# Other visits for the conversion of w1 in the first attention

## Chip, cores, metric

One Trainium2 chip, one of its cores. The metric is the device time of one execution in microseconds (us); lower is better. Line numbers (L...) are those of the kernel before.

## The reference

Hash attention over 4 batches x 8 heads, 768 positions, head size 64, then a Fourier mixing block with a two-layer perceptron.

```python
q_bits = (q @ proj > 0); k_bits = (k @ proj > 0)        # 6 bits each
mask = bucket(q_bits)[:, :, :, None] == bucket(k_bits)[:, :, None, :]
scores = where(mask, q @ k.T / 8, -1e9)
attn = softmax(scores) @ v                              # (4, 8, 768, 64)
x = attn.transpose(0, 2, 1, 3).reshape(4, 768, 512)
u = x + real(fft(fft(x, axis=1), axis=2))
un = (u - mean(u)) / sqrt(var(u) + 1e-6)
out = u + relu(un @ w_ch1) @ w_ch2                      # 512 -> 2048 -> 512
```

w_ch1 (512 x 2048) and w_ch2 arrive as 64-bit floats and are narrowed to 32 bits on the chip.

## The kernel before

The kernel goes through the four batches. `attention(b)` handles a batch as four pairs of heads; pair n (n = 4b + t) is six steps, one for each block of 128 keys, c = 0 to 5, and after each step the generator yields. In this text such a yield of `attention(0)` is a **visit**: i = 6t + c, 24 of them.

A step does, for its block of keys: scores of all 768 queries for both heads (PE, L897 and L905), two halves g into two PSUM buffers; the exponential of each half (ACT, L916); the values of the step before (PE, L941); and a running sum of the exponentials (DVE, `acc`, L1026, not for c = 0 and c = 5). In the first five pairs the mask is put into the scores: the key and query bits, computed on PE (L812), are turned by DVE into the tile `qkb` (L816, L822, L828) and enter by the matmuls of L897. So the scores of pair n+1 cannot start before DVE has written its `qkb`.

The closing of pair n falls into steps 0 and 1 of pair n+1, function `scale`: after the last values, ACT copies the output out (L952, L955), PE sums the weights over the keys (L960), DVE turns that sum and takes its reciprocal (`rt`, `rc`: L967, L969, L970). One step later ACT spreads the reciprocal (`rr`, eight copies, L978) and DVE turns it again and multiplies (L983, L987).

`prepare(n+1)` runs inside pair n, one piece per step from c = 1: turn q (DVE, L779); the norm of q (ACT, L761, which reads the loaded q) and turn k; the norm of k, and the bits of q; the bits of k. `load(n+1)`, the DMAs for q (eight, L576), k (four, L568) and v (two, L562) of the next pair, is issued on SP's queue at the start of pair n. q and k of two pairs share buffers, so `load(n+1)` also needs that `prepare(n)` has finished reading.

Beside the attention runs `weights1`, the conversion of w1: 16 slices of 128 x 512, in the order f outer (four column blocks), c inner (four row blocks). Each `next` on it converts one slice (`narrow`): on DVE L639, L643 and, after ACT's L647, L649; on ACT L647, L654, L655. It then issues the fetch (SP, L704, 512 KB) of the slice seven further on, into the same raw buffer; there are seven raw buffers, three in the tile `zraw` and four in the tile `fraw`. `zraw` lies where `fold` later writes its `z` (from visit 21 on), `fraw` where `mix(0)` writes `F`. A fetch waits until DVE and ACT have read the buffer.

When the four slices of a column block f < 1024 are done, the next `next` starts `average(f)`: PE sums the block (`ws`, L664; four products, one for each row block, the last of which needs the last slice), ACT copies the sum (`part`, L669), and then the next slice is converted. The `next` after that does the mean (`wm`, PE, L672) and subtracts it (`centre`, DVE, L678, four operations) ahead of its slice. The two column blocks from 1024 on are averaged after the attention.

Which visit calls `next` is said in the main program: `if i % 5 < 4`. The part from `prepare(0)` to the late averages stands under `manual_schedule`, so each engine works through its instructions in the order in which the program issues them.

Of the kernel before, what the change touches and what calls it, by code (L numbers as in the profile page):

```python
# [26 lines left out]
NPAIR = H // 2  # L27
# [458 lines left out]
def _main(  # L486
# [27 lines left out]
    def wt(shape, dtype, tag, name, bufs=2):  # L514
        return work.tile(shape, dtype, tag=tag, name=name, bufs=bufs)
# [4 lines left out]
    def pt(shape, name):  # L520

        turn[0] += 1
        if roomy[0] and turn[0] % 2:
            if turn[0] % 4 == 1:
                return ps_o.tile(shape, F32, tag="o", name=name)
            return ps_sc.tile(shape, F32, tag="sc", name=name)
        return ps_1.tile(shape, F32, tag="ps", name=name)
# [147 lines left out]
    def centre(f, avg):  # L675
        for c in range(NDC):
            w = w1[:, c, f : f + WC]
            nc.vector.tensor_tensor(w, w, avg, op=ALU.subtract)  # L678
# [43 lines left out]
    def weights1():  # L722
        slices = [
            (w1[:, c, f : f + WC], moe_w_ch1[c * P : (c + 1) * P, f : f + WC])
            for f in range(0, DFF, WC)
            for c in range(NDC)
        ]
        zt = wt([P, 3, 2 * WC], F32, "z", "zraw1", 1)
        ft = wt([P, 12, WC], F32, "F", "fraw", 1)
        raws = [zt[:, i] for i in range(3)] + [  # L730
            ft[:, i : i + 2].rearrange("p i w -> p (i w)") for i in range(0, 8, 2)
        ]
        arrival = Arrival(slices, raws, 0, nc.sync)
        for i in range(arrival.depth):
            arrival.fetch(i)
            if i == 2:
                load(1)
        yield
        half = None
        for i in range(len(slices)):  # L740
            arrival.convert(i, ft[:, 8 + i % 4].bitcast(I32))
            yield
            if half:
                centre(half[0], next(half[1]))
                half = None
            if i % NDC == NDC - 1:


                f = i // NDC * WC
                if f < DFF // 2:  # L750
                    half = f, average(f)
                    next(half[1])
# [6 lines left out]
    def norm(n, io, tn):  # L759
        junk = wt([P, S], BF16, "junk", f"sq{io}_{n}", 1)  # L760
        nc.scalar.activation(  # L761
            junk, tn, AF.Square,
            accum_out=norms[:, io, n : n + 1],
        )

    def prepare(n):

        lite = n in LITE
        ts = {}
        for io, nm in enumerate("qk"):  # L770
            tn = nat.pop((nm, n))
            tt = wt([P, S], F32, nm + "t", f"{nm}t{n}")
            if n > 0:
                to, at = tt, tn
                if nm == "q":

                    to = tt.rearrange("p (i r n) -> p r i n", i=2, r=2)
                    at = tn.rearrange("p (r i n) -> p r i n", i=2, r=2)
                nc.vector.transpose(to, at)  # L779
            for g in range(2) if n == 0 else ():  # L780
                ps = pt([P, 3, P], f"tr{nm}{n}_{g}")
                for i in range(3):
                    c = 2 * i + g if nm == "q" else 3 * g + i
                    nc.tensor.transpose(ps[:, i, :], tn[:, c * P : (c + 1) * P], ident)
                if nm == "q":
                    for i in range(2):
                        dst = tt[:, i * HALF + g * HALF // 2 : i * HALF + (g + 1) * HALF // 2]
                        evac(
                            dst.rearrange("p (j c) -> p c j", c=3),
                            ps[:, :, i * D : (i + 1) * D],  # L790
                        )
                else:
                    evac(
                        tt[:, g * HALF : (g + 1) * HALF],
                        ps.rearrange("p c t -> p (c t)"),
                    )
            ts[nm] = tt
            yield
            norm(n, io, tn)
        if lite:  # L800

            qk = wt([P, 2, S], BF16, "qb", f"qkb{n}")
            qz = qk[:, 0].rearrange("p (g s) -> p g s", g=2)
            bits = {"q": qz[:, 0], "k": qk[:, 1, 0:HALF]}
            for io, nm in enumerate("qk"):
                ps = pt([P, HALF], f"bits{nm}{n}")
                for j in range(4):  # L810
                    h, g = divmod(j, 2)
                    nc.tensor.matmul(  # L812
                        ps[32 * j : 32 * j + 32, :], pjw[:, h * D : h * D + 32],
                        ts[nm][:, g * HALF : (g + 1) * HALF], start=True, stop=True,
                    )
                nc.vector.tensor_scalar(  # L816
                    bits[nm], ps, 0.0, off[:, io : io + 1],
                    op0=ALU.is_gt, op1=ALU.subtract,
                )
                if io == 0:  # L820
                    for g in (1, 0):
                        nc.vector.tensor_scalar(  # L822
                            qz[:, g], qz[:, 0], own[:, g : g + 1], None, op0=ALU.mult
                        )
                else:
                    for j in range(4):
                        to, at = (slice(32 * i, 32 * i + 32) for i in (j, j ^ 1))
                        nc.vector.tensor_copy(qk[to, 1, HALF:S], qk[at, 1, 0:HALF])  # L828
                yield
            preps[n] = ts["q"], ts["k"], qk, None  # L830
            return

        ps = pt([P, HALF], f"bits{n}")
        for j in range(4):
            src = ts["qk"[j // 2]][:, (j % 2) * HALF : (j % 2 + 1) * HALF]
            nc.tensor.matmul(
                ps[32 * j : 32 * j + 32, :], pj, src, start=True, stop=True
            )
        bt = wt([P, HALF], BF16, "bt", f"bt{n}")
        nc.vector.tensor_scalar(bt, ps, 0.0, None, op0=ALU.is_gt)  # L840
        yield

        qb = wt([P, 2, S], BF16, "qb", f"qb{n}")
        kb = wt([P, 2, NT], F32, "kb", f"kb{n}")
        for h in range(2):
            ps = ps_sc.tile([P, 2, 512], F32, tag="sc", name=f"qb{n}_{h}")
            for g in range(2):
                rows = slice(32 * g, 32 * g + 32)
                with behind() if g + h else nullcontext():
                    last[0] = nc.tensor.matmul(  # L850
                        ps[:, g, 0:HALF], pw[rows, h, :], bt[rows, :],
                        start=True, stop=True,
                    )
            evac(qb[:, h, :].rearrange("p (g s) -> p g s", g=2), ps[:, :, 0:HALF])
        ps = ps_sc.tile([P, 2, 512], F32, tag="sc", name=f"kb{n}")
        for c in range(NT):
            g, i = divmod(c, NT // 2)
            rows = slice(64 + 32 * g, 96 + 32 * g)
            with behind() if c else nullcontext():
                last[0] = nc.tensor.matmul(  # L860
                    ps[:, g, 2 * i : 2 * i + 2], bt[rows, i * P : (i + 1) * P],
                    pw[rows, :, 0], start=True, stop=True,
                )
        nc.vector.tensor_copy(
            kb.rearrange("p h (g i) -> p g i h", g=2),
            ps[:, :, 0:NT].rearrange("p g (i h) -> p g i h", h=2),
        )
        preps[n] = ts["q"], ts["k"], qb, kb
# [674 lines left out]
    with tc.manual_schedule(engines={ET.PE, ET.DVE, ET.Activation, ET.Pool, ET.SP}):  # L1543
        for _ in prepare(0):
            pass
        roomy[0] = False
        for i, _ in enumerate(attention(0)):
            if i == 2 * NT - 1:
                nc.sync.dma_start(ch, cn["ch"].ap())
                nc.sync.dma_start(sq, cn["sq"].ap())  # L1550
            if i % 5 < 4:
                next(other, None)
        for _ in other:
            pass
        pwf = wt([P, 2, P], F32, "ef", "pwf", 1)
        nc.sync.dma_start(pwf, cn["pw"].ap())
        nc.scalar.copy(pw, pwf)
        means = []
        late = [(f, average(f)) for f in range(DFF // 2, DFF, WC)]
        for _, avg in late:  # L1560
            next(avg)
        for f, avg in late:
            means.append((f, wt([P, WC], F32, "u", f"mean{f}", 2)))
            nc.scalar.copy(means[-1][1], next(avg))
# [94 lines left out]
```

## Time and profile before

| what | us |
|---|---|
| median of 3 runs | 1078.12 (1077.32 to 1079.49) |
| the profiled execution | 1079.54 |
| its span | 1077.8 |

So 1.74 us of the profiled execution lie around its span, and it is 1.42 us above the median. Over the span PE is busy 96%, DVE 73%, ACT 46%.

The first exponential of each pair of the first attention starts, in the timeline of ACT, at:

| pair | 0 | 1 | 2 | 3 | 4 (second attention) |
|---|---|---|---|---|---|
| us | 12.95 | 37.26 | 65.07 | 88.77 | 120.83 |

In the timeline a row gives start, length, engine, line, operation, output<-input, count, and in brackets how long the engine sat idle before it and what released it. Busy shares of a whole span mix stages with different limits: what a change in the first 120 us is worth is read there. A row of SPq is an issue of DMAs; its length is the time SP spent on issuing.

### The profile page before, as it was taken

The page shows a single profiled execution, that of the slowest core. Times are in us where ns is not written, and L with a number is a line of the kernel's source. Part 1 is how long each engine was busy: PE and PEld are TensorE (multiplying, and loading weights), DVE is VectorE, ACT ScalarE, POOL GpSimd, SP SyncE. Part 2 cuts the span into 40 slices and gives each one's busy share as a digit, 9 for nine tenths or more (in the row PEclk, how much of TensorE's full clock was granted, in tenths as well). Part 3 has the DMA queues.
Part 4 walks back from the last instruction along what each step waited for, and adds up shares of the span by engine and source line. Part 5 has one row for each costly group of instructions (what it writes and reads, how often), then busy time and mean ns, then how long its engine had stood idle before and what let it go on. Part 6 is the DMA issues. An engine that isn't in the chain of part 4 may idle for free.

```text
span 1077.8 us, 14130 instructions
## 1 busy us (share of the span) xinstructions
PE 1034.6 (96%) x4933; PEld 633.4 (59%) x4933; DVE 786.7 (73%) x1336; ACT 500.4 (46%) x1055; POOL 59.3 (5%) x132
## 2 busy tenths in 40 slices
PE   7989899999999999999999999999999999999997
PEld 3333364447644585545664575645675579668576
DVE  5899969896789977777858876776856875644353
ACT  6988554762287323455336424354325522440420
POOL 0000000011000020010000020010000012200000
PEclk9999999999999999999999999999999999999998
DMA  8764452370154461224062233222033204222301
GB/s 200 206 141 78 99 143 54 122 237 9 29 131 169 136 187 37 52 64 88 11 191 73 64 104 116 50 66 66 15 111 96 69 23 173 61 78 90 125 20 42
DMA packets 175710, 103.13 MB, mean 96 GB/s; under 512 B 129552, under 2 KB 162960, under 8 KB 175632
## 3 DMA queue, kind: packets, MB, share of 16 engines
q1 hardware_dynamic: 169840, 88.65, 30.6%
q0 software_dynamic: 4224, 13.11, 3.7%
q8 instruction: 41, 0.67, 0.3%
q10 hardware_dynamic: 1568, 0.39, 0.2%
q14 instruction: 37, 0.30, 0.1%
HBM read 81.14 MB, written 20.97 MB: 95 GB/s over the span
## 4 chain that ended last, share of the span: by engine, by line
PE 72%; DVE 17%; ACT 6%; issue 2%; DMA 1%; SPq 1%; DVEq 0%; ACTq 0%
PE o L1335 26%; PE h_p L1456 22%; PE oo L941 8%; PE sc L905 7%; DVE acc L1026 3%; DVE pk L930 2%; PE cs L1147 2%; ACT pk L916 2%; PE A L1176 2%; PE B L1176 1%; DMA kn<-in_k_dram 1%; ACT rr L978 1%; DVE x L1190 1%; PE sum L960 1%; SPq L576 1%
## 5 line engine op out<-in xcount | busy, mean ns | idle before, releaser
L1335 PE MATMUL o<-w,h 128*128 128x256 f32 x1152 | 260.0, 383 | 0.8 <-DVE w L1347 0.6
L1335 PEld LDWEIGHTS o<-w,h 128*128 128x128 f32 x1152 | 217.8, 191 | 41.8 <-issue 6.5
L916 ACT ACTIVATE pk<-sc 128x768 f32<-128x768 f32 x192 | 147.4, 809 | 78.2 <-PE oo L941 33.3
L1456 PE MATMUL h_p<-x,w 128*128 128x384 f32 x448 | 164.5, 494 | 3.1 <-ACT h L1478 1.6
L905 PE MATMUL sc<-qt,kt 64*128 64x384 f32 x768 | 154.9, 505 | 3.1 <-ACT pk L916 2.8
L930 DVE SCALAR_TENSOR_TENSOR pk<-qb,kb,pk 128x768 f32<-128x768 bf16 x132 | 128.7, 1012 | 39.0 <-ACT pk L916 38.4
L941 PE MATMUL oo<-pk,vn 128*64 128x385 f32 (+1 forms) x768 | 146.4, 495 | 1.1 <-DVE pk L930 0.6
L1456 PEld LDWEIGHTS h_p<-x,w 128*128 128x128 f32 x448 | 82.0, 190 | 69.3 <-issue 9.9
L1026 DVE TENSOR_TENSOR acc<-acc,pk 128x1536 f32<-128x1536 f32 (+1 forms) x72 | 105.8, 1483 | 5.3 <-ACT pk L916 5.1
L1456 PE MATMUL h_p<-w 128*128 128x384 f32 x288 | 106.1, 490 | 0.1
L941 PEld LDWEIGHTS oo<-pk,vn 128*64 128x64 f32 x768 | 50.5, 136 | 87.0 <-issue 72.6
L905 PEld LDWEIGHTS sc<-qt,kt 64*128 64x128 f32 x768 | 66.5, 187 | 55.7 <-issue 18.4
L1456 PEld LDWEIGHTS h_p<-w 128*128 128x128 f32 x288 | 53.6, 190 | 39.6 <-ACT w L1493 2.4
L1365 ACT COPY tq<-o 128x256 f32<-128x256 f32 x24 | 8.9, 373 | 104.8 <-PE o L1335 104.8
L1347 DVE SCALAR_TENSOR_TENSOR w<-o,rs,w 128x256 f32<-128x256 f32 x56 | 26.6, 479 | 41.2 <-PE o L1335 41.2
L1335 PE MATMUL o<-w 128*128 128x256 f32 x176 | 42.2, 383 | 0.2 <-DVE w L1347 0.2
L1489 DVE TENSOR_TENSOR h<-h 128x384 f32<-128x384 f32 x32 | 17.8, 555 | 29.6 <-ACT h L1488 29.6
L1085 POOL DMA_DIRECT2D out_dram<-w x30 | 16.4, 548 | 407.6 <-issue 314.6
L1335 PEld LDWEIGHTS o<-w 128*128 128x128 f32 x176 | 32.9, 190 | 7.5 <-DVE w L1347 1.2
L1354 ACT COPY tq<-o 128x256 f32<-128x256 f32 x24 | 8.8, 368 | 60.3 <-PE o L1335 60.1
L1381 DVE TENSOR_TENSOR tq<-tq,o 128x256 f32<-128x256 f32 x24 | 10.0, 418 | 36.4 <-PE o L1335 36.4
L1482 DVE TENSOR_TENSOR h<-h 128x384 f32<-128x384 f32 x32 | 17.7, 552 | 21.8 <-ACT h L1481 21.7
(170 smaller groups left out, 1334.5 us busy)
## 6 DMA issues: line engine op xcount, KB each, us to landing
w<-ad SPq DMA_DIRECT2D x168, 128.0 KB, 2.0
w<-bd SPq DMA_DIRECT2D x42, 512.0 KB, 4.4
zraw<-in_moe_w_ch_dram POOLq DMA_DIRECT2D x16, 512.0 KB, 4.4
bd<-w SPq DMA_DIRECT2D x14, 512.0 KB, 3.3
vn<-in_v_dram SPq DMA_DIRECT2D x32, 192.0 KB, 3.5
qn<-in_q_dram SPq DMA_DIRECT2D x120, 48.0 KB, 2.4
kn<-in_k_dram SPq DMA_DIRECT2D x60, 96.0 KB, 3.0
zraw<-in_moe_w_ch_dram SPq DMA_DIRECT2D x8, 512.0 KB, 7.4
```

Of the source, the lines that this page charges most:

```text
L905: last[0] = nc.tensor.matmul(ps[:, h, 0:HALF], kt[rows, ks], qt[rows, qs], start=kb is not None, stop=True,)
L916: done_by[ET.Activation] = nc.scalar.activation(pk[:, g, :, 0:HALF], ps[:, :, 0:HALF], AF.Exp, scale=SCALE)
L930: done_by[ET.DVE] = nc.vector.scalar_tensor_tensor(w, qb[:, h].rearrange("p (g s) -> p g s", g=2), kb[:, h, c : c + 1], w, op0=ALU.is_equa ...
L941: oo = nc.tensor.matmul(oos[g][h * D : (h + 1) * D, 0:w], nat["v", n][:, (2 * c + h) * D : (2 * c + h + 1) * D], pk[:, g, h, 0:w], start=( ...
L1026: done_by[ET.DVE] = nc.vector.tensor_tensor(acc[:, g], (first if c == 1 else acc)[:, g], new[:, g], op=ALU.add,)
L1147: nc.tensor.matmul(ps[:, pc + 2 * lo : pc + 2 * hi - 1 : 2], z[:, cp, pc, par, t * P : (t + 1) * P], ch[:, cp, pc, lo:hi], start=(cp == 0) ...
L1176: nc.tensor.matmul(ps[:, cols], F[:, par, k, t, j * P : (j + 1) * P], sq[:, t, k, cols], start=(t == 0), stop=(t == 1),)
L1335: nc.tensor.matmul(ps, a[:, r], right7[i][:, r], start=start and r == 0, stop=r == HF // 2 - 1, skip_group_check=not start,)
L1347: nc.vector.scalar_tensor_tensor(t[:, cols], src, r, t[:, cols], op0=ALU.mult, op1=ALU.add)
L1456: nc.tensor.matmul(ps, left[:, k], right[i][:, k], start=start and k == 0, stop=k == 1, skip_group_check=not start,)
L1482: done_by[ET.DVE] = nc.vector.tensor_tensor(c21, c12, c21, op=ALU.add)
L1489: done_by[ET.DVE] = nc.vector.tensor_tensor(c22, c21, c22, op=ALU.add)
```

## The change

Three edits.

1. The visits that call `next` are listed. Converted slices by visit:

| pair | before (visit: slice) | after |
|---|---|---|
| 0 | 0:0 1:1 2:2 3:3 5:4 | 0:0 1:1 2:2 4:3 5:4 |
| 1 | 6:5 7:6 8:7 10:8 11:9 | 8:5 9:6 10:7 11:8 |
| 2 | 12:10 13:11 15:12 16:13 17:14 | 14:9 15:10 16:11 17:12 |
| 3 | 18:15 | 20:13 21:14 22:15 |

`average(0)` starts at visit 5 in both, its `centre` comes at visit 6 before and 8 after; `average(512)` starts at visit 10 before and 11 after, its `centre` at 11 before and 14 after. Fetches move with the conversions: the last one (slice 15, issued by slice 8's conversion) goes from visit 10 to visit 11, behind the loads of the tables `ch` and `sq` and directly ahead of `load(3)`.

2. For the pairs 2, 3 and 4, the norm of q is issued with the turning of q (step 1 in place of 2), and the norm of k with the turning of k (step 2 in place of 3).

3. The four raw buffers in `fraw` are used first, the three in `zraw` after them.

```diff
@@ weights1
-        raws = [zt[:, i] for i in range(3)] + [
+        raws = [
             ft[:, i : i + 2].rearrange("p i w -> p (i w)") for i in range(0, 8, 2)
-        ]
+        ] + [zt[:, i] for i in range(3)]
@@ prepare
             ts[nm] = tt
+            soon = 1 < n <= NPAIR
+            if soon:
+                norm(n, io, tn)
             yield
-            norm(n, io, tn)
+            if not soon:
+                norm(n, io, tn)
@@ main program
+        turns = {0, 1, 2, 4, 5, 8, 9, 10, 11, 14, 15, 16, 17, 20, 21, 22}
         for i, _ in enumerate(attention(0)):
             if i == 2 * NT - 1:
                 nc.sync.dma_start(ch, cn["ch"].ap())
                 nc.sync.dma_start(sq, cn["sq"].ap())
-            if i % 5 < 4:
+            if i in turns:
                 next(other, None)
```

No instruction is added or removed. In the built programs the order on each engine differs up to the first steps of the second attention (about 140 us in the trace before); from there it is the same on PE, DVE and ACT.

## Prediction

> **What bounds the kernel now.** I read the busy shares first, then the same by stretches of 30 us, then the timelines of DVE, PE, ACT and SP's queue where the order changes.
>
> ```profile
> PE 1034.6 (96%) x4933; PEld 633.4 (59%) x4933; DVE 786.7 (73%) x1336; ACT 500.4 (46%) x1055; POOL 59.3 (5%) x132
> ```
>
> PE bounds the whole. But by stretches (columns: us, then busy us with instruction counts for PE, PEld, DVE, ACT, POOL; granted PE clock; DMA share; GB/s):
>
> ```profile
> 30.00:60.00 30.00, 26.54 (x180) 10.52 (x181) 26.85 (x44) 24.05 (x48) 0.00 (x0) 1.00 0.63 160
> 60.00:90.00 30.00, 27.68 (x182) 10.79 (x180) 28.27 (x51) 29.41 (x59) 0.00 (x0) 1.00 0.60 128
> 90.00:120.00 30.00, 26.89 (x185) 9.39 (x181) 27.34 (x52) 19.58 (x47) 0.11 (x1) 0.94 0.43 84
> ```
>
> In the first attention PE idles 2.3 to 3.5 us in 30, and DVE is hardly freer. DVE's timeline shows four idle times from 17 to 138 us:
>
> ```profile
> 17.80 1.83 DVE L1026 TENSOR_TENSOR acc<-pk,pk 128x768 f32<-128x768 f32 x2 [1.67 <-ACT pk L916]
> ...
> 39.12 0.58 DVE L967 STREAM_TRANSPOSE rt<-sum 128x384 f32<-128x384 f32 x1 [2.00 <-PE sum L960]
> ...
> 72.83 0.98 DVE L983 STREAM_TRANSPOSE rt<-rr 128x768 f32<-128x768 f32 x1 [0.28 <-ACT rr L978]
> ...
> 118.73 0.98 DVE L983 STREAM_TRANSPOSE rt<-rr 128x768 f32<-128x768 f32 x1 [1.73 <-ACT rr L978]
> ...
> 137.40 0.55 DVE L840 TENSOR_SCALAR bt<-bits 128x384 bf16<-128x384 f32 x1
> ```
>
> Between 17.80 and 137.40 DVE works without a break but for 2.00 + 0.28 + 1.73 us. At 138.00 PE starts again right after that last row (idle 0.65, released by `bt`), and from there to 171 its timeline lists no idle time. So the first 138 us are one DVE queue, and the rest is PE without slack: **every microsecond that DVE idles more before `bt` is a microsecond at the end.** The change removes no DVE work and `bt` has the same work before it; only those idle times can change. At most 4.0 us can be won.
>
> **The change, step by step.** Prices, from rows: a conversion takes 1.85 us of DVE (48.95 to 50.80) and 2.2 of ACT (35.03 to 37.26); both exponentials 1.45 of ACT; scores 1.72, values 1.44, the two sums 1.43 of PE (34.39, 36.11, 37.55, 38.98); `centre` 2.4 of DVE; `qkb` of k 1.74 of DVE (33.40 to 35.14).
>
> *Pair 0 to 1.* Slice 3 moves from visit 3 to 4: on DVE behind `acc` and the `qkb` of k. DVE, never idle here, still ends slice 4 at 37.1. But the fourth product of `ws` needs slice 3:
>
> ```profile
> 33.39 1.06 PE L664 MATMUL ws<-w,ones 128*32 128x512 f32 x8
> 34.39 0.34 PE L897 MATMUL sc<-qkb 64*128 64x384 bf16 x2
> ```
>
> Before, slice 3 is done at 31.7. After, DVE ends `qkb` of q at 29.85, then `acc` 1.75, `qkb` 1.74, slice 3 1.85: 35.2. The fourth product ends at 35.5, scores 37.2, values 38.65, sum 40.1 (no `wm` between): `rt` can start at 40.15, not 39.12. **+1.1.** Behind `ws`, ACT's queue holds `part`, slice 4, then the exponentials of pair 1, which come at 38.35 (before 37.26); behind slice 4 SP's queue holds its refetch and then `load(2)`.
>
> *Pair 1, steps 1 and 2.* `centre` and two conversions have left, so DVE runs dry. ACT: exponentials 38.35, output 39.75, step 1's exponentials as PE delivers, 41.0 to 42.5, `rr` to 44.2. DVE ends `rc` at 41.15, waits 0.65 for the first exponential and 0.7 for `rr`, turns, multiplies, ends at 46.0. **+1.35.** q is then the next thing:
>
> ```profile
> 37.76 5.35 SPq L576 DMA_DIRECT2D qn<-in_q_dram  x8
> 43.16 2.17 SPq L568 DMA_DIRECT2D kn<-in_k_dram  x4
> ```
>
> 1.1 later, its last part is issued about 43.9 and lands 2.3 us after (the median of those rows is 2.5): 46.2. DVE waits 0.2. The norm of q (1.0) now stands ahead of step 2's exponentials, 47.15 to 48.65; DVE, done turning q at 47.1, waits 0.9 for the first. **+1.1.** Nothing is idle after that: turn k, `centre`, slices 5 to 8, ending at 67.0.
>
> *Pair 1 to 2* is pair 0 to 1 again, larger:
>
> ```profile
> 57.70 1.07 PE L664 MATMUL ws<-w,ones 128*32 128x512 f32 x8 [1.22 <-DVE qkb L816]
> ```
>
> After, the last product waits for slice 7 at the end of step 4: from 48.0 `acc` (1.75), k (0.9), `centre`, slice 5 (54.9), `acc`, `qkb` of q (1.3), slice 6 (59.8), `acc`, `qkb` of k (63.3), slice 7: 65.15. PE has had no other work since about 61. Then scores 67.1, values 68.55, sum 70.0, while DVE, out of work at 67.0, waits 3.05 (before: nothing). **+3.05.**
>
> *Pair 2, steps 1 and 2.* As in pair 1, 0.65 + 0.65, less the 0.28 lost before: **+1.0**, multiplication done at 75.9. Now SP's queue decides:
>
> ```profile
> 63.35 0.42 SPq L1549 DMA_DIRECT2D ch<-k_ch  x1
> 63.82 0.42 SPq L1550 DMA_DIRECT2D sq<-k_sq  x1
> 64.29 8.12 SPq L576 DMA_DIRECT2D qn<-in_q_dram  x8
> ```
>
> After, `load(3)` stands behind slice 15's fetch, which waits for ACT's slice 8 (`part` 66.05, conversion, 68.3). The issue of the eight takes 3.92 us with free queues (the row at 77.34), 8.12 behind three half-megabyte loads; with `ch` and `sq` some 3 us ahead I take 6.8: last issue 75.7, landed 77.9, k at 80.9. DVE waits 2.0, then 0.85 for the exponentials. **+2.85**; by the fastest issue 0.85, by the slowest 4.2.
>
> *Pair 3.* DVE ends slice 12 at 98.6, PE's sum at 98.3: no wait. 0.35 + 0.7 in step 1: **+1.05**. Then no idle to the end; slices 13 to 15, two more than before, are DVE work carried over, about 3.7 us.
>
> *Raw buffers in another order:* nothing. It lets `zraw` be free (slice 13, visit 20) when `fold` writes there at visit 21; otherwise `z` would wait for slice 15. `F`, now bound to slice 15 (about 127), is first copied into by ACT at 132.72 before, 12 later after: covered. The last two averages follow slice 15 in PE's queue; DVE has work meanwhile.
>
> *Clock.* After PE idled 112.4 to 116.6 with one `ws` in it, it was granted 0.59 and 0.56 in the four us that followed:
>
> ```profile
> 114.00:116.00 2.00, 1.06 (x8) 0.16 (x8) 1.90 (x6) 0.00 (x0) 0.00 (x0) 1.00 0.74 152
> 116.00:118.00 2.00, 1.41 (x8) 0.20 (x8) 0.94 (x3) 0.92 (x5) 0.00 (x0) 0.59 1.11 209
> 118.00:120.00 2.00, 2.00 (x11) 0.65 (x7) 1.23 (x2) 1.94 (x8) 0.00 (x0) 0.56 0.89 129
> ```
>
> PE's idle 1.93 at 73.9 cost no clock. The new wait before the last `ws` product (61 to 65) is of the first size, and what follows it leads to `rt`. Four us at 0.57 lose 1.8; it may fall before or after a window's edge: I take **+0.9**, ends 0 and 1.8.
> [...]
>
> **Sum:** 1.1 + 1.35 + 1.1 + 3.05 + 1.0 + 2.85 + 1.05 + 0.9 = 12.4. On the profiled execution, 1079.54: 1091.9; that one lies 1.42 above the median of the runs, so 1090.5 in their terms.
>
> **Rivals.**
> *Shallow:* only the two waits for `ws` are real (1.1 + 3.05); loads come in time and the short waits of steps 1 and 2 close up: 1082.3, up to 1086. For it: PE, ACT and DVE sit within a microsecond of each other there, and my error in each is near that. Against: the row at 64.29 shows SP issuing q for 8 us.
> *Deeper:* `load(3)` takes 8.12 behind the tables and the clock halves at both pair boundaries: +1.35, +0.9 and up to +1.8 more: 1092.5 to 1096.
> *No change:* the waits for `ws` are harmless because DVE catches up: 1078. Against: DVE has nothing spare before 138.
> *Faster:* the limit in steps 1 and 2 is ACT, not DVE. PE's waits for exponentials there are 1.60 (48.04) and 1.93 (75.84):
>
> ```profile
> 75.84 0.34 PE L897 MATMUL sc<-qkb 64*128 64x384 bf16 x2 [1.93 <-ACT pk L916]
> ```
>
> Both stand behind a conversion that ACT does after `rr`; the change takes it away. If DVE follows, it wins 2.0 + 0.28 and part of the 1.73: 1075. It decides only if DVE's idle time before `bt` falls under 4.0 us, so DVE would have to find other work at the boundary; its order there offers none.
> *The change doesn't do what it says:* the built order shows the conversions at the new visits; no chance given.
>
> **Chances.** Forecast (1086 to 1092.5) 0.55, shallow 0.2, deeper 0.14, no change 0.05, faster 0.06. This measurement tells 0.2% (2.2 us) from no change: faster 0.06, same 0.05, slower 0.89. Range 1082 to 1096, which leaves out the last two cases and the tails; the likeliest gives 1090.5.
>
> **What would show it.** DVE's `rt` (L967) after waits of 3.1 and 3.0 us at the first two boundaries, with `ws` on PE released by DVE's conversion; first exponentials of pairs 1, 2 and 3 at 38.4, 68.3 and 95.2; DVE's `bt` near 149; two waits for `qn`; a clock near 0.6 after 65. It is wrong if DVE's idle time from 17.8 to `bt` is not about 15.5 us, or if PE after `bt` has slack that takes it up.

## The result and the profile after

| | before | after |
|---|---|---|
| median of the timed runs, us | 1077.72 (4 runs) | 1090.20 (1089.94 to 1092.46, 4 runs) |
| ratio, 95% interval | | 1.0112 (1.0100 to 1.0124) |
| profiled execution / its span, us | 1079.54 / 1077.8 | 1092.46 / 1090.5 |
| DVE's start of `bt`, us | 137.40 | 152.12 |
| DVE's idle time from the first `acc` to `bt`, us | 4.0 | 18.35 |

The change costs 12.5 us by the medians. The profiled execution after is the slowest of its four (the other three lie at 1089.9 to 1090.3), and from profile to profile the cost is 12.9. Lines of the changed kernel from L797 on stand four to five further down: `acc` is L1030, `rt` L971 and L987, `bt` L844, the exponential L920.

DVE's timeline after, the rows with idle time in the first attention (start, length, line, count; in brackets the idle time before it and what ended it):

```profile
37.51 0.69 DVE L649 CUSTOM_DVE_ANT_0 w<-w,fraw 128x1024 uint16<-128x1024 uint16 x1 [1.25 <-ACT fraw L647]
40.96 0.58 DVE L971 STREAM_TRANSPOSE rt<-sum 128x384 f32<-128x384 f32 x1 [2.75 <-PE sum L964]
42.70 1.83 DVE L1030 TENSOR_TENSOR acc<-pk,pk 128x768 f32<-128x768 f32 x2 [0.69 <-ACT pk L920]
45.05 0.98 DVE L987 STREAM_TRANSPOSE rt<-rr 128x768 f32<-128x768 f32 x1 [0.52 <-ACT rr L982]
48.73 1.83 DVE L1030 TENSOR_TENSOR acc<-acc,pk 128x768 f32<-128x768 f32 x2 [0.63 <-ACT pk L920]
...
69.11 0.69 DVE L649 CUSTOM_DVE_ANT_0 w<-w,fraw 128x1024 uint16<-128x1024 uint16 x1 [2.12 <-ACT fraw L647]
74.59 0.58 DVE L971 STREAM_TRANSPOSE rt<-sum 128x384 f32<-128x384 f32 x1 [4.80 <-PE sum L964]
76.34 1.83 DVE L1030 TENSOR_TENSOR acc<-pk,pk 128x768 f32<-128x768 f32 x2 [0.69 <-ACT pk L920]
78.69 0.98 DVE L987 STREAM_TRANSPOSE rt<-rr 128x768 f32<-128x768 f32 x1 [0.53 <-ACT rr L982]
80.58 0.97 DVE L779 STREAM_TRANSPOSE qt<-qn 128x768 f32<-128x768 f32 x1
...
101.97 0.58 DVE L971 STREAM_TRANSPOSE rt<-sum 128x384 f32<-128x384 f32 x1 [1.42 <-PE sum L964]
103.71 1.83 DVE L1030 TENSOR_TENSOR acc<-pk,pk 128x768 f32<-128x768 f32 x2 [0.69 <-ACT pk L920]
106.06 0.98 DVE L987 STREAM_TRANSPOSE rt<-rr 128x768 f32<-128x768 f32 x1 [0.53 <-ACT rr L982]
...
134.13 0.98 DVE L987 STREAM_TRANSPOSE rt<-rr 128x768 f32<-128x768 f32 x1 [1.73 <-ACT rr L982]
...
152.12 0.55 DVE L844 TENSOR_SCALAR bt<-bits 128x384 bf16<-128x384 f32 x1
```

The brackets add up to 18.35 us, 14.3 more than before, and `bt` starts 14.7 later. The same three steps repeat in each pair: the sum at the boundary, the first exponentials, `rr`. `qt` at 80.58 has no bracket: q was there.

What delays the sum stands in PE's timeline:

```profile
32.95 1.06 PE L664 MATMUL ws<-w,ones 128*32 128x512 f32 x6
35.25 1.04 PE L664 MATMUL ws<-w,ones 128*32 128x512 f32 x2 [1.24 <-DVE w L649]
...
61.17 1.06 PE L664 MATMUL ws<-w,ones 128*32 128x512 f32 x6
65.97 1.92 PE L664 MATMUL ws<-w,ones 128*32 128x512 f32 x2 [3.74 <-DVE w L649]
```

Three products of the block sum run when PE reaches them, the fourth waits for DVE's slice, at 35.25 and 65.97. At the second place PE's clock halves; windows of 2 us (us, then busy us of PE, PEld, DVE, ACT, POOL; granted clock; DMA share; GB/s):

```profile
64.00:66.00 2.00, 0.03 (x1) 0.03 (x1) 1.83 (x4) 0.00 (x0) 0.00 (x0) 0.82 0.00 0
66.00:68.00 2.00, 2.00 (x4) 0.34 (x6) 0.95 (x2) 0.07 (x1) 0.00 (x0) 0.50 0.80 248
68.00:70.00 2.00, 2.00 (x10) 1.20 (x10) 0.69 (x1) 1.94 (x4) 0.00 (x0) 0.50 1.00 384
70.00:72.00 2.00, 2.00 (x8) 0.52 (x8) 0.00 (x0) 2.00 (x4) 0.00 (x0) 0.50 0.90 320
```

After `bt` the shift stays fixed. Two rows of PE's timeline, the same instruction before and then after:

```profile
375.11 1.05 PE L905 MATMUL sc<-qt,kt 64*128 64x384 f32 x4 [1.59 <-ACT pk L916]
```

```profile
389.82 0.92 PE L909 MATMUL sc<-qt,kt 64*128 64x384 f32 x4 [1.59 <-ACT pk L920]
```

They stand 14.7 apart, with the same idle time before them. Just behind this place the trace before has the clock at 0.72 and 0.85 for two windows of 4 us (from 374), the trace after has 1.00. That gives back 1.65 us: from 382 us of the trace before to its last product PE stands 13.05 later, and the spans end 12.7 apart.

### The profile page after: what moved, and what is told of

Same layout as the page of the kernel before. It is cut to its first block, busy times and chain, and to the rows that moved or that the text cites. A ratio compares the mean times of both kernels' runs of the same rounds, so it can differ in the third digit from the quotient of the medians.

```text
span 1090.5 us, 14124 instructions
## 1 busy us (share of the span) xinstructions
PE 1038.9 (95%) x4933; PEld 633.2 (58%) x4933; DVE 787.4 (72%) x1336; ACT 500.7 (46%) x1055; POOL 61.2 (6%) x132
## 4 chain that ended last, share of the span: by engine, by line
PE 71%; DVE 17%; ACT 5%; DMA 2%; issue 2%; SPq 2%; DVEq 0%; ACTq 0%
PE o L1339 26%; PE h_p L1460 22%; PE oo L945 8%; PE sc L909 7%; DVE acc L1030 3%; DVE pk L934 2%; PE cs L1151 2%; PE A L1180 2%; SPq L576 2%; ACT pk L920 2%; PE B L1180 1%; DMA kn<-in_k_dram 1%; DVE x L1194 1%; DVE w L643 1%; ACT rr L982 1%
## 5 line engine op out<-in xcount | busy, mean ns | idle before, releaser
L920 ACT ACTIVATE pk<-sc 128x768 f32<-128x768 f32 x192 | 147.5, 808 | 86.8 <-PE sc L909 41.6
L1030 DVE TENSOR_TENSOR acc<-acc,pk 128x1536 f32<-128x1536 f32 (+1 forms) x72 | 106.0, 1486 | 6.0 <-ACT pk L920 5.8
L1493 DVE TENSOR_TENSOR h<-h 128x384 f32<-128x384 f32 x32 | 17.8, 556 | 29.9 <-ACT h L1492 29.9
L1151 PE MATMUL cs<-ch,z 128*128 128x128 f32 (+3 forms) x192 | 31.6, 316 | 2.1 <-DVE z L1125 1.5
```

What stands on the lines that cost most here:

```text
L920: done_by[ET.Activation] = nc.scalar.activation(pk[:, g, :, 0:HALF], ps[:, :, 0:HALF], AF.Exp, scale=SCALE)
L1030: done_by[ET.DVE] = nc.vector.tensor_tensor(acc[:, g], (first if c == 1 else acc)[:, g], new[:, g], op=ALU.add,)
L1151: nc.tensor.matmul(ps[:, pc + 2 * lo : pc + 2 * hi - 1 : 2], z[:, cp, pc, par, t * P : (t + 1) * P], ch[:, cp, pc, lo:hi], start=(cp == 0) ...
L1493: done_by[ET.DVE] = nc.vector.tensor_tensor(c22, c21, c22, op=ALU.add)
```

## The experiments

The medians of the kernel before in these sessions are 1078.3 to 1079.0; ratios are against them. "Idle" is DVE's idle time between its first `acc` and `bt`, from the profile.

**Edit 2 alone** (the kernel before with the norms moved).

```diff
+            soon = 1 < n <= NPAIR
+            if soon:
+                norm(n, io, tn)
             yield
-            norm(n, io, tn)
+            if not soon:
+                norm(n, io, tn)
```

> The kernel before with edit 2 alone (the norms of pairs 2 to 4 with the turnings). DVE-queue theory: step 2's exponentials come 1.0 us later in pairs 1 to 3, but DVE gets to their sums later still (50.8, 77.5 and 99.7 against 49.7, 77.4 and 99.1), so DVE idles no more and the time stays: 1077.7, within 1 us. Rival, the chain of exponentials on ACT sets the pace: 1.0 in each of three pairs, 1080.7.

Measured 1082.01, ratio 1.0033 (1.0022 to 1.0043), idle 7.8: 1.3 above the rival's time. The size is near the rival's, the cause neither's. ACT's timeline in pair 2, and PE's:

```profile
74.80 0.84 ACT L761 ACTIVATE sq<-qn 128x768 bf16<-128x768 f32 x1 [1.45 <-DMA qn<-in_q_dram]
```

```profile
78.62 0.51 PE L901 MATMUL sc<-qkb 64*128 64x384 bf16 x2 [4.17 <-ACT pk L920]
```

Ahead of step 2's exponentials the norm waits for q's load; PE, left idle for 4.17 us, gets half clock for 6.8 us (0.86 and three times 0.50 in the windows from 76 to 84), and the scores, bits and sum behind it come late for DVE. I had left both the load and the clock out of this expectation.

**Edit 3 alone** (the kernel before with the raw buffers of `fraw` first; the diff is that of the change).

> The kernel before with edit 3 alone (the raw buffers of fraw first). Both theories: nothing, within 1 us of the kernel before. If the order of the buffers mattered for the arrival of the first slices, step 0 to 2 of pair 0 would be late by the difference, 0.5 us or more.

Measured 1078.79, ratio 1.0002 (0.9993 to 1.0012). No effect on the time.

**The change without edit 2** (the norms where they were before).

> The changed kernel with edit 2 undone. DVE-queue theory: in pair 1 step 2's exponentials no longer wait for the norm of q and its load, so DVE's 0.63 us wait there goes and nothing else: 1089.6, within 1 us of the changed kernel's 1090.2. Rival, the norms hold up steps 1 and 2 of each pair: 2.5 to 4 us less, 1086 to 1087.7.

Measured 1092.09, ratio 1.0127 (1.0111 to 1.0144), beside 1.0112 (1.0100 to 1.0124) for the whole change: nothing is won back, and the expected 1089.6 was missed by 2.5 us. DVE's wait before the sums of step 2 is gone from its profile, as expected. That profiled execution took 1089.37, the other three 1091.9 to 1092.5, so it does not show what made those slower. So edit 2 costs 3.5 us on its own and nothing that can be told on top of edit 1. A reason is seen in pair 2 of the changed kernel, where the norm of q at 78.68 has no wait for the load before it, as the boundary was late already; that this is the whole of it is not shown.

The profile of this run shows the clock's part in the second boundary:

```profile
65.43 1.91 PE L664 MATMUL ws<-w,ones 128*32 128x512 f32 x2 [4.30 <-DVE w L649]
```

The wait is longer than the 3.74 us of the changed kernel, but the half clock behind it lasts 3.4 us here and 6.8 there. PE takes 7.2 us from this product to the sum, against 8.6 there and 5.7 at the first boundary, at full clock.

**One slice moved** (the kernel before, slice 3 at visit 4).

```diff
-            if i % 5 < 4:
+            if i == 4 or i != 3 and i % 5 < 4:
```

> The kernel before with one slice moved: slice 3 at visit 4 in place of 3, all else as before. Theory: ws waits for slice 3 at 35.2, slice 4's conversion on DVE waits 1.25 for ACT behind part, the sum comes 1.8 later; DVE idles 4.0 in place of 2.0 at that boundary, then has centre and slice 5 as before and loses nothing more: 1079.7. Rival, DVE catches up by the next boundary: 1077.7.

Measured 1080.06, ratio 1.0012 (1.0003 to 1.0022): 1.6 us, within 0.4 of the expected 1079.7. DVE's timeline shows the two waits of the changed kernel. After them it has the two waits for `rr` that the kernel before has too, and one more that the expectation lacked, 0.97 us for the sum at 94.88, at pair 3:

```profile
37.25 0.69 DVE L649 CUSTOM_DVE_ANT_0 w<-w,fraw 128x1024 uint16<-128x1024 uint16 x1 [1.26 <-ACT fraw L647]
40.68 0.58 DVE L967 STREAM_TRANSPOSE rt<-sum 128x384 f32<-128x384 f32 x1 [2.74 <-PE sum L960]
```

This is the first boundary by itself: 1.26 + 2.74 in place of 2.00. The rival, DVE catching up, falls: `bt` comes 2.6 later.

**The block sum later** (the changed kernel; `ws` starts one conversion later).

```diff
             yield
-            if half:
+            if half and i % NDC == 0:
+                next(half[1])
+            elif half:
                 centre(half[0], next(half[1]))
                 half = None
...
                     half = f, average(f)
-                    next(half[1])
```

> The changed kernel with the block sum (ws) started one conversion later, in step 2 of the next pair (visits 8 and 14), mean and centre one visit after it. Theory, the waits come from ws standing in PE's queue behind a slice that DVE converts late: DVE's idle at the first two boundaries falls from 4.0 and 6.9 us to about 1 each, the half clock after 65 us goes, so 9 to 11 us come back: 1079 to 1081. Rival, DVE runs dry because conversions were taken out of steps 0 and 1: the wait moves from the sum to rr and the exponentials, 1086 or more.

Measured 1091.92, ratio 1.0125 (1.0108 to 1.0142). The waits at the boundaries fell as the theory said, to 0.52 and 0. The time did not:

```profile
78.31 0.98 DVE L780 STREAM_TRANSPOSE qt<-qn 128x768 f32<-128x768 f32 x1 [5.01 <-DMA kn<-in_k_dram]
```

SP's queue in the same run:

```profile
64.52 0.33 SPq L704 DMA_DIRECT2D fraw<-in_moe_w_ch_dram  x1
64.90 0.94 SPq L1555 DMA_DIRECT2D ch<-k_ch  x1
65.89 0.42 SPq L1556 DMA_DIRECT2D sq<-k_sq  x1
66.42 0.36 SPq L704 DMA_DIRECT2D fraw<-in_moe_w_ch_dram  x1
66.83 9.25 SPq L576 DMA_DIRECT2D qn<-in_q_dram  x8
```

`load(3)` stands behind a fetch that waits for DVE and behind four large loads, and issuing its eight parts takes 9.25 us, to 76.1. In the changed kernel the issue ends at 76.6, no earlier, but there DVE comes to q only at 80.58: the late block sum covered the load. Take the sum away and the load is the next thing late. I had priced the load in the prediction and forgot it here. The rival's time, 1086 or more, holds, and its cause in part: of the 15.7 us of idle time 6.7 are two waits for q (1.68 in pair 1 and the 5.01), and 6.8 are waits for exponentials and `rr` in pairs 1 to 3, 2.5 more than in the changed kernel.

**Fetches on another queue.** Two runs: with the block sum later, all of w1's fetches on POOL's queue; then only the refetches, the first seven on SP.

```diff
-        arrival = Arrival(slices, raws, 0, nc.sync)
+        arrival = Arrival(slices, raws, 0, nc.gpsimd)
```

> The run with the later block sum, and besides w1's fetches issued on POOL's queue in place of SP's, so that the loads of q and k stand behind no fetch. Theory, taking the block sum out of the way uncovered the load: DVE's waits for q of 1.68 and 5.01 us go, PE's wait of 5.50 and the half clock after it with them; 6.7 us less than the 1091.9 of that run: 1085, between 1083.5 and 1086.5. Rival, steps 1 and 2 run dry whatever is late: the waits go over to the exponentials, 1089 or more.

```diff
-                    self.queue.dma_start(raw.bitcast(I64), src)
+                    (self.queue if i < self.depth else nc.gpsimd).dma_start(
+                        raw.bitcast(I64), src
+                    )
```

> The run with the later block sum, the first seven fetches on SP as there, only the nine refetches on POOL's queue. Theory: the late start of the run with all fetches on POOL (its first acc at 23.5 in place of 17.7) goes, the loads of q and k still stand behind no fetch, DVE idles 5.9 us from the first acc to bt (4.0 in the kernel before): 1080 to 1082. What is left over the kernel before, some 2 to 3 us, is the dryness of steps 0 and 1. Rival, the gain of that run came from the fetches' own timing: 1085 or more.

Measured 1087.42, ratio 1.0075 (1.0058 to 1.0091), and 1083.19, ratio 1.0035 (1.0022 to 1.0049). Both lie above their ranges, by 0.9 and 1.2 us. The waits for q are gone from both, idle is 5.93 and 5.95. In the first run DVE's first `acc` comes at 23.5 in place of 17.7, a late start that was not in its expectation. In the second these idle times are left in DVE's timeline for pair 1, and the same two in pairs 2 and 3:

```profile
39.29 1.83 DVE L1033 TENSOR_TENSOR acc<-pk,pk 128x768 f32<-128x768 f32 x2 [0.69 <-ACT pk L923]
41.65 0.98 DVE L990 STREAM_TRANSPOSE rt<-rr 128x768 f32<-128x768 f32 x1 [0.53 <-ACT rr L985]
```

So with the block sum and the load out of the way about 8 of the 12.5 us are gone. The three waits of 1.2 in step 1 are left, but the boundary's wait is down to 0.55 from the 2.00 of the kernel before, so DVE idles only 1.9 more than there. The timed runs go from 1080.9 to 1085.9, and the profiled one is the fastest; its profile doesn't show what slows the others.

**POOL for the centring** (the kernel before): the last two means, then all four.

```diff
-            nc.vector.tensor_tensor(w, w, avg, op=ALU.subtract)
+            (nc.gpsimd if f >= DFF // 2 else nc.vector).tensor_tensor(
+                w, w, avg, op=ALU.subtract
+            )
```

> The kernel before with the eight subtractions of the last two means (0.6 us each on DVE, at 122 to 134 us) on POOL. If the first 138 us are one DVE queue, bt comes up to 4.8 us earlier: 1073 to 1076. Rival, that stretch is held by the exponentials and PE as well, or POOL slows DVE at the memory: 1077 or more.

> The kernel before with all 16 subtractions of means on POOL; ACT copies each of the first two means (0.6 us) out of PSUM. DVE-queue theory: a further 2 x 2.4 us off DVE before 68 us: 1069 to 1073. Rival, ACT is as full there as DVE (35 to 55 us without a break), and the two copies and the shared stretch give it back: 1074 or more.

Measured 1087.21, ratio 1.0071 (1.0053 to 1.0088), and 1087.84, ratio 1.0084 (1.0068 to 1.0101): the theory missed by 11 and 15 us. The rivals' "or more" holds both times, and of the reasons given only the remark that POOL slows DVE fits the profile. POOL and DVE in the first run:

```profile
123.25 11.74 POOL L678 TENSOR_TENSOR w<-w,mean 128x512 f32<-128x512 f32 x8 [27.53 <-ACT mean L1566]
```

```profile
123.84 5.33 DVE L1123 TENSOR_TENSOR z<-ef 128x190 f32<-128x190 f32 x4
```

One subtraction takes POOL 1.47 us, and while POOL works DVE's four operations of `fold` take 5.33 us; before they take 1.16. What POOL took off DVE came back, and more, as slower work of DVE: its work up to `bt` is 119.8 us in place of 115.6, though 4.8 us of subtractions had left it. DVE also waits 1.64 and 1.88 us more for exponentials, just ahead of `bt`.

**Towards a faster kernel** (the kernel before): with the later block sum and refetches on POOL's queue; with the last two centres issued six steps later, which puts four subtractions behind `bt`; with both.

```diff
-                if b == 1 and i == 2:
+                if b == 1 and i == 8:
```

> The kernel before (its own visits) with the later block sum and the refetches on POOL's queue. Theory: it has the DVE work of steps 0 and 1 that the change took away, and neither wait to lose; of its 2.0 us at the first boundary about 0.8 go: 1077 to 1078.5, not slower. Rival, refetches on POOL's queue cost DVE or the loads time: 1080 or more.

> The kernel before with the last two centres issued later, so that one of them (four subtractions, 2.4 us of DVE) stands behind bt, where DVE idles. If the stretch to bt is one DVE queue, bt comes up to 2.4 us earlier; PE waits only 1.4 us there, so 1076.5 to 1078. Rival, the rest of the stretch waits for exponentials: no change, 1078.3.

> The two before together: 1075.5 to 1078. Rival as there: 1078 or more.

Measured 1084.01, ratio 1.0037 (1.0023 to 1.0050); 1078.34, ratio 0.9989 (0.9979 to 0.9999); 1084.91, ratio 1.0046 (1.0032 to 1.0059). The first and the third missed and lie where their rivals have them. In the first run's profile (1081.29) DVE idles 7.0 us: 1.48 for an exponential of pair 1, and 1.42 at the last boundary after PE had half clock from 89 on; its timed runs are slower still, which is left open. With the refetches on POOL's queue the old visits (1084.01) and the new ones (1083.19, above) can't be told apart: their intervals nearly coincide. So on top of those two edits the change costs nothing that can be told, while the two edits cost the kernel before 5 us, for a reason that no profile here shows in full.

The second lies 0.3 above its range and on its rival's number, 1078.3. Against the 1078.99 of the kernel before in the same session it is 0.6 us faster, with an interval that just leaves out 1; it is the only run ahead of both kernels. Its profile shows both at work: DVE's work up to `bt` is 2.3 us less, but it idles 1.4 more, 0.99 of it for an exponential, and `bt` comes 0.8 earlier, at 136.59.

**The runs in one number.** Start of `bt` less start of the first `acc`, less DVE's idle time between, is DVE's work in that stretch: 115.6 us before, 116.0 after, 116.7, 115.7, 116.5, 115.6 and 116.7 in the first five experiments as told, 116.2 and 116.4 in the two with fetches on POOL's queue, 115.8 in the kernel before with both those edits, and 113.3 and 113.4 where 2.4 us of it were moved behind `bt`. But for those two it is the same to 1.2 us, while the idle time goes from 4.0 to 18.35. The two runs with POOL's subtractions fall out, with 119.8 and 120.1.

Behind `bt` the traces of all these runs can be laid over the one before, since PE has the same products in each. From 145 to 375 us of the trace before, a run's lateness changes by 0.4 us or less from one end to the other, by 1.0 in the run with all fetches on POOL's queue. At 376 it falls by 1.6 us in the ten profiles that have no half clock there, and by nothing in the three that have it, as the kernel before has. So a microsecond on PE just behind `bt` is one at the end, and profiles of one kernel can still differ by that 1.6.

## Why the prediction was right, step by step

*DVE's queue sets the first 138 us, and PE without slack the rest:* shown by the constant work above and by the fixed shift of 14.7 us from `bt` to 390 us. That the total came out to 0.3 us (1090.5 predicted, 1090.20 measured) is in part luck, as the steps show.

| step (DVE idle, after less before) | predicted | measured |
|---|---|---|
| pair 0 to 1 | 1.1 | 2.0 |
| pair 1, steps 1 and 2 | 2.45 | 1.84 |
| pair 1 to 2, with the clock | 3.95 | 6.92 |
| pair 2, step 1 | 1.0 | 0.94 |
| pair 2, step 2 (q's load) | 2.85 | 0 |
| pair 2 to 3 | 0 | 1.42 |
| pair 3, step 1 | 1.05 | 1.22 |
| sum | 12.4 | 14.34 |

*The boundaries:* the mechanism was right, the size too small, for two reasons. I let the fourth product of `ws` take a quarter of the four; alone it takes 1.04 us. And the half clock lasted 6.8 us: from the start of the last `ws` product to the start of `rt` PE took 5.7 us at the first boundary and 8.6 at the second, so the clock cost 2.9, not 0.9 and not the 1.8 of its upper end. DVE's waits of 1.25 and 2.12 for ACT's L647, which stands behind `part`, were not in my account either, but they add nothing: they lie beside PE's way to the sum, which has no idle time from the fourth product on, and without them DVE would have waited that much longer for the sum.

*The clock* I had at 0.9, with ends 0 and 1.8, from the 0.59 and 0.56 granted behind 116 us of the trace before. That a window's edge decides between the ends is shown by no run. In the changed kernel the clock was at half around this wait for 6.8 us, twice the 3.4 us that the trace before shows from 116.4 on. In the run without edit 2 it lasted 3.4 and cost 1.5, within my ends. The length of the wait alone doesn't tell: in the changed kernel 2.63 us before 95.60 went with half clock, 3.07 us before 127.81 did not.

*q's load in pair 2:* predicted 2.85, measured 0. The load itself came as predicted (last issue at 76.3, predicted 75.7), but DVE came to it at 80.58, not at 75.9, mainly because the two boundaries before it took 3.9 us longer than I had them. The run with the later block sum shows that the price was there, 5.01 us, hidden behind another wait. I added two waits that lie beside each other.

*Steps 1 of pairs 1 to 3:* 0.65 and about 0.7 predicted (0.35 and 0.7 in pair 3), 0.69 and 0.52 measured. In step 2 of pair 1 I had 1.1 for q's load and the norm; DVE waited 0.63, and not for q.

*Pair 2 to 3:* nothing predicted, 1.42 measured. PE had waited 2.63 for `qkb` and got half clock for 3.4 us. I had put the clock at one place only.

*After `bt`:* 2.0 us came back in a stretch that I had called rigid: 1.65 since the half clock of 376 us didn't return, and 0.3 behind PE's last product.

*Its own signs:* first exponentials of pairs 1 to 3 at 39.0, 70.6 and 97.1 (38.4, 68.3 and 95.2 predicted), `ws` released by DVE and the clock at half after 65 as said, `bt` at 152.1, not 149, and one wait for q's load, 2.05 us on ACT at 47.07, not two. It called itself wrong if DVE's idle time were not about 15.5 us (a figure that leaves out its own 0.9 for the clock) or if PE took time up after `bt`. The idle time was 18.35, and 2.0 us were taken up. So by these two tests the account was wrong in its sizes, though the path it named is the one the traces show.

So the total, 12.4 against 12.5, hides errors that cancel: boundaries 5.3 too small, the load 2.85 too large, and 2 us given back late. *The rivals:* faster and no change fell, since DVE had no other work to take up; shallow is below the result; the deeper one named a second stretch of half clock rightly, though it came at the boundary from pair 2 to 3, and not its load, which took 5.56 us to issue, not 8.12.

## What to carry to other kernels

When one engine is busy without a break through a stage, price a new order by that engine's idle time alone, and ask at each place where it will run dry. Work that is moved to where an engine has time also moves what waits for it: here a block sum in PE's queue behind the last slice, and the loads in SP's queue behind a fetch. Waits that lie beside each other don't add; taking one away uncovers the next, so change both before judging either.

## What the hardware showed that I had not expected

A wait of PE cost nearly as much again in the clock: 3.74 us of idle time before the `ws` product at 65.97, 6.8 us at 0.50 from 65.3 on, 2.9 us lost. Ahead of PE's last product the trace before has half clock for 3.4 us from 116.4 and from 375.8, the trace after for 6.8 from 65.3 and for 3.4 from 96.0; with edit 2 alone there are 6.8 from 77.4. Which length follows a wait I could not tell from the wait's own. Differences between executions of one kernel go with the granted clock: of the 49 of the kernel before in the three later sessions, the 22 with a mean of 0.996 or less average 1079.6 us, the 27 with more 1078.1.

POOL's subtraction on 128x512 takes 1.47 us, against 0.60 on DVE, and it slows DVE: four operations of DVE took 5.33 us in place of 1.16 beside it. What makes DVE slower there, at the memory or elsewhere, no run here tells.
